# Causal attention, a gated layer and routed experts on one core: half of the attention pairs copy P by DMA into a float32r tile and transpose it from there, two banks in one run

## The chip, the cores and the metric

One core of a Trainium2 chip runs the whole kernel. The metric is the device time of one execution in microseconds (us), as a median of several runs. TensorE (PE) does the matmuls, VectorE (DVE), ScalarE (ACT) and GpSimd (POOL) work on their results, SyncE (SP) issues the DMAs.

## What is computed

Three layers in a row, here with b = 0..3, 12 heads of 64, 448 positions and a width of 768:

```python
scores = where(causal, q @ k.T / 8, -1e9)            # layer 1: plain causal attention
x = softmax(scores) @ v                              # heads side by side: (4, 448, 768)

theta = x @ w_theta                                  # layer 2
y = w_tok_r @ (x * cos(theta)) + w_tok_i @ (x * sin(theta))
u = x + y;  x = u + relu(u @ w_ch)

w = softmax of the two largest of x @ w_gate         # layer 3: 4 experts, each one head of 64
for e in range(4):
    out += (w[e] where e was chosen) * (softmax(causal(x @ wq[e] @ (x @ wk[e]).T / 8)) @ (x @ wv[e]) @ wo[e])
```

## The kernel before

Everything is held transposed (features on partitions, the 448 positions along the row), and heads come in pairs: two heads of 64 fill 128 partitions. Layer 1 has six pairs for each b (`attn1`), layer 3 two pairs of experts for each b (`attn2`): 32 pairs in all. Between them `dense1` does layer 2 and the projections of layer 3.

The dense matmuls take float32r operands, each number split into a high and a low part of which three products are summed (`mm3`). Their weights are converted once for b = 0, written to a scratch in HBM, and read back from there for every b as tiles `unit`, six buffers of them, by DMAs in SP's queue. SP's queue also brings q and k of a pair (`raw`) and v (`vt`), and stores the result.

One call of `pair` does attention for two heads:

- `scores([2])`: the scores of the third block of 128 positions of both heads, float32 matmuls on one half of the array's rows for each head, side by side, into two banks `sc`. Then the scores of the last 64 positions of both heads together, then `scores([1, 0])`.
- `softmax`: VectorE adds the mask and finds the row's extreme, ScalarE takes the exponential and the sum, into P (`pa`, one tile for each head, and `pc` for the last positions). `norm` scales P by the reciprocal sums, on GpSimd or ScalarE.
- P is transposed in blocks of 128 by 128, four to a PSUM bank `tp`, four banks a pair (`banks`), 16 transposes: P's block is the stationary operand, the identity the moving one, both float32. Each bank is copied to a tile `ph` by ScalarE or VectorE as soon as its four are there.
- `av`: 16 float32 matmuls, each head on one half of the array's columns, and the result is split into high and low (`hl`).

The order of instructions on each engine is not that of the program. `Plan` collects steps with a due time and costs of its own (`cost`, `LATENCY`, `DMA_RATE`), and `issue` writes each engine's queue in the order of a list schedule: at each point an engine takes the ready step of the earliest due time whose buffers are free. The table `K` sets the due times. On the chip each queue then runs strictly in the order written. Attention for the next b is meant to stand between the matmuls of the dense layers of this b. Since all instructions are written by one helper, all have line 478 in the profile, and tiles tell them apart.

Of the kernel before, what the change touches and what calls it, by code (L numbers as in the profile page):

```python
# [23 lines left out]
P = 128  # L24
# [94 lines left out]
ANY = {"cmb", "cv"}  # L119
# [6 lines left out]
class Plan:  # L126
# [16 lines left out]
    def cost(self, engine, name, out, ins, kw):  # L143
        n = out.width if isinstance(out, View) else 0
        psum = any(v.root.psum for v in ins)
        if engine == "tensor":
            n = ins[1].width
            if name != "matmul":
                return 109.0
            if ins[1].dtype != F32:  # L150
                return max(52.0, 8.0 + 0.43 * n)
            if self.mode(ins, name):
                return 8.0 + 0.86 * n
            return 16.0 + 1.72 * n
# [36 lines left out]
    def add(self, engine, name, *args, **kw):  # L191
# [8 lines left out]
        if isinstance(self.block, Step) and self.block.engine == engine:  # L200
            step = self.block
            step.cost += cost
        else:
            step = Step()
            step.calls, step.engine, step.cost, step.options, step.done = [], engine, cost, [], []
            step.deps, step.users, step.tiles, step.fresh = {}, [], [], []
            step.soft, step.heirs = {}, []
            step.order = len(self.steps)
            step.due = self.due
            step.lag = 0.0  # L210
            step.mode = self.mode(ins, name) if engine == "tensor" else 0
# [100 lines left out]
    def issue(self):  # L312
# [62 lines left out]
        while count < len(self.steps):  # L375
# [13 lines left out]
            for e in order:  # L389
# [4 lines left out]
                for x in avail[e]:  # L394
# [86 lines left out]
class Engine:  # L481
# [3 lines left out]
    def __getattr__(self, method):  # L485
# [3 lines left out]
K = {"path": 1.62, "hop": -40.0, "slack": 10.0, "war": 300.0, "ahold": 41360.0, "f1": 0.03, "f2": 0.91, "f3": 1.13,  # L489
# [7 lines left out]
def dense_sparse_attention_kernel(ctx: ExitStack, tc: tile.TileContext, qk, v, w64, w32, wo, wvg, wtok, out):  # L497
# [10 lines left out]
            "qp": 3, "v2": 4, "pa": 3, "pc": 2, "ph": 3, "cmb": 2, "st": 9, "gt": 2, "sm": 2}  # L508
# [13 lines left out]
    pool.identity(ident)  # L522
    mask = const([512], F32, "mask")
# [82 lines left out]
    def pair(raw, vts, gate, dest, due, gap, tag=lambda name: name):  # L606
# [21 lines left out]
        def scores(chunks):  # L628
            banks = [pst("sc") for _ in range(2)]
            plan.group()  # L630
            at = 0
            for c in chunks:
                n = 128 * (c + 1)
                for j in range(2):
                    pe.matmul(banks[j][:, at:at + n], qs[j][:, 128 * c:128 * c + 128], ks[j][:, :n], start=True, stop=True)
                at += n
            plan.end_group()
            at = 0
            for c in chunks:
                n = 128 * (c + 1)  # L640
                for j in range(2):
                    softmax(banks[j][:, at:at + n], part(j, c), n, mask[:, 512 - n:512], 2 * (2 - c) + j)
                at += n
# [9 lines left out]
        scores([2])  # L653
# [5 lines left out]
        scores([1, 0])  # L659
# [3 lines left out]
        def blk(who, c, kc):  # L663
            if who == 2:
                return pc[:, kc * 128:kc * 128 + 128]
            return ps[who][:, SECS[c] + kc * 128:SECS[c] + kc * 128 + 128]
# [3 lines left out]
        parts = [sbt([1024], F32, tag("ph")) for _ in range(2)]  # L670
        for t, i, blocks in banks:
            tp = pst("tp")
            at = 0
            for who, c, kc in blocks:
                if who == 2:
                    pe.transpose(tp[:, at:at + 128], blk(who, c, kc), ident)
                    at += 128
                else:
                    place = tp[:, at:at + 256].rearrange("p (h j d) -> p h j d", h=2, j=2)
                    pe.transpose(place[:, :, who], blk(who, c, kc), ident)  # L680
                    at += 256 * who
            plan.copy(parts[t][:, 512 * i:512 * i + 512], tp)
# [11 lines left out]
        plan.completes(o_[:, :S])  # L694
        if dest is not None:
            plan.copy(dest, o_[:, :S])
        h_ = sbt([S], F32R, "hl")
        l_ = sbt([S], F32R, "hl")
# [7 lines left out]
    def attn1(b, due0, gap):  # L706
        for pr in range(H // 2):
# [22 lines left out]
            xhl[b, pr] = pair(fetch, [vt[:, j] for j in range(2)], None, xp, due, gap, tag)  # L730
# [162 lines left out]
    def attn2(b, due0, gap):  # L893
        qps, v2, g7 = st2[b]
        hl = []
        for r in range(2):
            due = due0 + r * gap
            hl.append(pair(lambda: qps[r], [v2[r][:, :, j] for j in range(2)], g7[:, r, :], None, due, gap))
        banks = K["wom"] if b == B - 1 else K["wo2"] if b == B - 2 else "a"
        names = {"a": "av", "m": "mm", "s": "sc", "t": "tp", "v": "av"}  # L900
        for m in range(NK):
# [6 lines left out]
            o = pst(names[banks[m % len(banks)]])  # L908
            i = 0
# [4 lines left out]
            ob = sbt([S], F32, "xt" if b == B - 1 else "cmb")  # L914
# [70 lines left out]
```

## Time and profile before

| | |
|---|---|
| Time, median of 3 runs | 675.54 us (674.79 to 676.07) |
| The profiled execution's own time | 675.52 us |
| Its span from the first to the last instruction | 673.7 us |
| Instructions | 11076, of them 3752 matmuls |
| TensorE busy | 645.6 us of the span |
| Granted clock of TensorE, mean | 0.991 |

The profiled execution stands at the median of the runs, so its parts can be added up to a time without any scaling. A busy TensorE in the profile means that some matmul is between its start and its modelled end; neighbours overlap, so what one costs in a row of them is read from the distance between starts, or from the chain of waits, where each piece holds the time that it alone took.

### The profile page before, as it was taken

The page shows a single profiled execution, that of the slowest core. Times are in us where ns is not written, and L with a number is a line of the kernel's source. Part 1 is how long each engine was busy: PE and PEld are TensorE (multiplying, and loading weights), DVE is VectorE, ACT ScalarE, POOL GpSimd, SP SyncE. Part 2 cuts the span into 40 slices and gives each one's busy share as a digit, 9 for nine tenths or more (in the row PEclk, how much of TensorE's full clock was granted, in tenths as well). Part 3 has the DMA queues.
Part 4 walks back from the last instruction along what each step waited for, and adds up shares of the span by engine and source line. Part 5 has one row for each costly group of instructions (what it writes and reads, how often), then busy time and mean ns, then how long its engine had stood idle before and what let it go on. Part 6 is the DMA issues. An engine that isn't in the chain of part 4 may idle for free.

```text
span 673.7 us, 11076 instructions
## 1 busy us (share of the span) xinstructions
PE 645.6 (96%) x3752; PEld 522.7 (78%) x3752; DVE 418.3 (62%) x1301; ACT 391.0 (58%) x977; POOL 111.3 (17%) x215
## 2 busy tenths in 40 slices
PE   7997679999999999999999999999999999999997
PEld 5664468778797879877887778788788888997875
DVE  4999999998955586543435677354633457434251
ACT  5999788768724482344557677543555364105374
POOL 3542212222200211000102134100100012001010
PEclk8999979999999999999999999999999999999999
DMA  8845630345788624245536442415541750063243
GB/s 332 282 140 193 241 125 29 110 150 176 273 257 277 220 100 149 88 139 162 166 93 236 154 141 67 139 46 173 148 132 48 229 172 23 24 220 116 64 156 134
DMA packets 46184, 103.13 MB, mean 153 GB/s; under 512 B 4784, under 2 KB 16560, under 8 KB 46128
## 3 DMA queue, kind: packets, MB, share of 16 engines
q1 hardware_dynamic: 46128, 102.43, 46.8%
q8 instruction: 29, 0.48, 0.3%
q14 instruction: 27, 0.22, 0.1%
HBM read 81.15 MB, written 21.26 MB: 152 GB/s over the span
## 4 chain that ended last, share of the span: by engine, by line
PE 83%; DVE 8%; ACT 6%; issue 1%; DMA 1%; POOL 0%; ACTq 0%; POOLq 0%; DVEq 0%
PE mm L478 54%; PE av L478 10%; PE sc L478 9%; PE tp L478 7%; PE cv L478 3%; ACT pa L478 2%; DVE cmb L478 2%; DVE zt L478 1%; ACT zn L478 1%; DVE pa L478 1%; DVE c L478 1%; DVE zn L478 1%; DMA unit<-scr 1%; ACT ph L478 1%; ACT pc L478 1%
## 5 line engine op out<-in xcount | busy, mean ns | idle before, releaser
L478 PE MATMUL mm<-zt,unit 128*128 128x448 f32 x720 | 161.1, 374 | 0.0
L478 ACT ACTIVATE pa<-pa,st 128x384 f32<-128x384 f32 (+2 forms) x262 | 125.3, 492 | 43.1 <-DVE st L478 37.6
L478 PEld LDWEIGHTS mm<-zt,unit 128*128 128x128 f32 x720 | 132.5, 188 | 17.3 <-issue 5.7
L478 PE MATMUL mm<-wt,zn 128*128 128x448 f32 x504 | 124.2, 380 | 0.5 <-ACT zn L478 0.5
L478 PE MATMUL mm<-hl,unit 128*128 128x448 f32 x432 | 103.5, 385 | 6.1 <-DVE zt L478 4.3
L478 PEld LDWEIGHTS mm<-wt,zn 128*128 128x128 f32 x504 | 90.4, 188 | 11.5 <-issue 2.0
L478 PEld LDWEIGHTS mm<-hl,unit 128*128 128x128 f32 x432 | 81.0, 193 | 20.2 <-DVE zt L478 5.5
L478 DVE CUSTOM_DVE_ANT_0 pa<-sc,mask 128x384 f32<-128x384 f32 (+1 forms) x174 | 67.0, 419 | 44.3 <-PE sc L478 37.6
L478 POOL TENSOR_SCALAR pa<-pa,st 128x256 f32<-128x256 f32 (+2 forms) x86 | 46.5, 550 | 256.9 <-DVE st L478 176.8
L478 ACT ACTIVATE ph<-tp 128x512 f32<-128x512 f32 x103 | 56.8, 593 | 44.4 <-PE tp L478 44.1
L478 PE MATMUL sc<-raw 64*128 64x384 f32 (+3 forms) x336 | 69.5, 437 | 2.0 <-DVE st L478 1.7
L478 PE MATMUL tp<-ident,pa 128*128 128x128 f32 x348 | 58.6, 275 | 5.0 <-POOL pa L478 4.1
L478 PEld LDWEIGHTS tp<-ident,pa 128*128 128x128 f32 x348 | 42.9, 141 | 13.0 <-POOL pa L478 5.3
L478 ACT ACTIVATE pc<-pc,st 128x448 f32<-128x448 f32 x56 | 37.4, 667 | 20.0 <-DVE st L478 19.5
L478 PE MATMUL av<-ph,vt 128*64 128x448 f32 (+3 forms) x384 | 46.8, 386 | 2.1 <-ACT xt L478 2.1
L478 PEld LDWEIGHTS av<-ph,vt 128*64 128x64 f32 x384 | 25.4, 136 | 27.4 <-issue 11.2
L478 PEld LDWEIGHTS sc<-raw 64*128 64x128 f32 (+1 forms) x336 | 33.8, 189 | 14.3 <-issue 5.9
L478 DVE TENSOR_TENSOR zn<-cv,zn 128x512 fp32r<-128x512 f32 (+1 forms) x48 | 29.8, 620 | 23.5 <-ACT zn L478 23.4
L478 PE MATMUL mm<-unit,zt 128*128 128x260 f32 (+1 forms) x288 | 40.7, 289 | 0.9 <-DMA unit<-scr 0.9
L478 ACT ACTIVATE zn<-cv 128x512 fp32r<-128x512 f32 (+1 forms) x36 | 19.5, 541 | 34.8 <-PE cv L478 34.7
L478 PEld LDWEIGHTS mm<-unit,zt 128*128 128x128 f32 (+1 forms) x288 | 36.1, 175 | 4.0 <-issue 1.8
L478 POOL MEMSET pc<- 128x64 f32 x32 | 5.0, 161 | 169.5 <-PE tp L478 169.4
(115 smaller groups left out, 893.9 us busy)
## 6 DMA issues: line engine op xcount, KB each, us to landing
unit<-scr SPq DMA_DIRECT2D x96, 384.0 KB, 3.5
scr<-unit SPq DMA_DIRECT2D x32, 384.0 KB, 3.2
raw<-qk SPq DMA_DIRECT2D x24, 480.0 KB, 4.3
c<-w SPq DMA_DIRECT2D x24, 384.0 KB, 3.3
vt<-v SPq DMA_DIRECT2D x24, 256.0 KB, 3.3
unit<-scr SPq DMA_DIRECT2D x18, 260.0 KB, 3.2
c<-scr SPq DMA_DIRECT2D x18, 256.0 KB, 2.8
out<-cmb SPq DMA_DIRECT2D x18, 224.0 KB, 2.7
```

Of the source, the lines that this page charges most:

```text
L478: getattr(getattr(self.nc, engine), name)(*args, **kw)
```

## The change

For 16 of the 32 pairs (layer 1 of b = 2 and 3, layer 3 of b = 1 and 2; `moved` is true), the blocks of P are copied by DMA from `pa` and `pc` into a new tile `bits` of type float32r, eight blocks to a tile and five DMAs to a tile, on SP's queue. The transposes read `bits` with a float32r identity, and write two banks `tp` in one run of eight; a pair has two such runs. The bits copied are those of the float32 numbers. `bits` takes its buffers from the tag `ph`, which has four of them now, before three. The other 16 pairs transpose as they did.

The rest concerns the order: the planner's price of a transpose, of a run on the new tile and of a change between parts of the array; a rule `stay`, by which TensorE, once it has done a step that uses a part of the array, prefers another such step that is ready and due within 4510 ns; `tp` banks taken in any order; some tiles claimed at an earlier step, and the six matmuls of the last projection kept together; and the table `K`, whose due times are all different. `joined` is false at both calls, so `scores` makes the same matmuls as before.

```diff
-ANY = {"cmb", "cv"}
+ANY = {"cmb", "cv", "tp"}
...
             if name != "matmul":
-                return 109.0
+                return 62.0 if ins[0].dtype != F32 else 109.0
...
+            if engine == "tensor" and name != "matmul" and ins[0].dtype != F32:
+                step.cost += 100.0
...
+                    if e == "tensor" and mode:
+                        if not s.mode:
+                            if pick is None:
+                                pick = x
+                            if due <= pick[0] + K["stay"]:
+                                continue
+                            break
+                        if pick is None or due <= pick[0] + K["stay"]:
+                            pick = x
+                        break
...
-                        end += 150.0
+                        end += 180.0
...
-K = {"path": 1.62, "hop": -40.0, "slack": 10.0, "war": 300.0, "ahold": 41360.0, "f1": 0.03, "f2": 0.91, "f3": 1.13,
-     "a0": 6370.0, "start": 56960.0, "d1": 25850.0, "g1": 13100.0, "gap": 15170.0, "gap1": 0.04, "gap2": -0.75, "len0":
...
+K = {"stay": 4510.0, "path": 1.7, "hop": -660.0, "slack": 10.0, "war": 300.0, "ahold": 36380.0, "f1": -0.01, "f2": 0.72,
+     "f3": 1.65, "a0": 4960.0, "start": 56770.0, "d1": 26990.0, "g1": 13110.0, "gap": 17410.0, "gap1": 0.36, "gap2":
...
-            "qp": 3, "v2": 4, "pa": 3, "pc": 2, "ph": 3, "cmb": 2, "st": 9, "gt": 2, "sm": 2}
+            "qp": 3, "v2": 4, "pa": 3, "pc": 2, "ph": 4, "cmb": 2, "st": 9, "gt": 2, "sm": 2}
...
+    identr = const([P], F32R, "identr")
+    dve.tensor_copy(identr, ident)
...
+            for p in ps:
+                plan.claim(p)
...
+        srcs = [x.rearrange("p (n j) -> p n j", j=128) for x in (ps[0], ps[1], pc)]
...
+        def move(t):
+
+            bits = sbt([8, 128], F32R, tag("ph"))
+            at = {}
+            x = 0
+            for i in (1, 0):
+                for who in range(3):
+                    todo = [(SECS[c] // 128 + kc if who < 2 else kc, (who, c, kc)) for w, c, kc in sets[t, i] if w == who]
+                    todo.sort()
+                    while todo:
+                        n = len(todo)
+                        step = todo[1][0] - todo[0][0] if n > 1 else 1
+                        while any(todo[k][0] != todo[0][0] + k * step for k in range(n)):
+                            n -= 1
+                        first = todo[0][0]
+                        sp.dma_start(bits[:, x:x + n].f32(), srcs[who][:, first:first + (n - 1) * step + 1:step])
+                        for k in range(n):
+                            at[todo[k][1]] = bits[:, x + k]
+                        x += n
+                        todo = todo[n:]
+            return lambda *key: at[key]
+
+        sets = {(t, i): blocks for t, i, blocks in banks}
+        groups = [((0, 1), (0, 0)), ((1, 1), (1, 0))] if moved else [((t, i),) for t, i, _ in banks]
+        for group in groups:
+            where = move(group[0][0]) if moved else block
+            tps = [pst("tp") for _ in group]
+            plan.group()
+            for tp, key in zip(tps, group):
+                at = 0
+                for who, c, kc in sets[key]:
+                    place = tp[:, at:at + 128]
+                    if who < 2:
+                        place = tp[:, at:at + 256].rearrange("p (h j d) -> p h j d", h=2, j=2)[:, :, who]
+                    pe.transpose(place.bitcast(F32R) if moved else place, where(who, c, kc), identr if moved else ident)
+                    at += 128 if who == 2 else 256 * who
+            plan.end_group()
...
+            plan.claim(parts[t])
+            for tp, (t, i) in zip(tps, group):
+                plan.copy(parts[t][:, 512 * i:512 * i + 512], tp)
...
-            xhl[b, pr] = pair(fetch, [vt[:, j] for j in range(2)], None, xp, due, gap, tag)
+            xhl[b, pr] = pair(fetch, [vt[:, j] for j in range(2)], None, xp, due, gap, False, b > 1, tag)
...
-            hl.append(pair(lambda: qps[r], [v2[r][:, :, j] for j in range(2)], g7[:, r, :], None, due, gap))
+            hl.append(pair(lambda: qps[r], [v2[r][:, :, j] for j in range(2)], g7[:, r, :], None, due, gap, False, 0 < b < B - 1))
```

## Rows read from the trace of the kernel before

**Rows 1.** The page, busy time of each engine: us, share of the span, instructions.

```profile
PE 645.6 (96%) x3752; PEld 522.7 (78%) x3752; DVE 418.3 (62%) x1301; ACT 391.0 (58%) x977; POOL 111.3 (17%) x215
```

**Rows 2.** Busy time by stretch; then granted clock, DMA share, GB/s.

```profile
60.00:112.00 52.00, 38.90 (x200) 29.12 (x198) 51.19 (x140) 40.61 (x92) 7.83 (x12) 0.93 0.41 139
...
215.00:340.00 125.00, 125.00 (x706) 104.16 (x704) 70.51 (x200) 63.44 (x155) 16.21 (x33) 1.00 0.48 156
...
380.00:480.00 100.00, 100.00 (x581) 81.56 (x578) 55.31 (x157) 56.92 (x135) 19.25 (x33) 1.00 0.38 119
```

**Rows 3.** TensorE's waits from 215 to 630 us: total, times, longest.

```profile
PE cv L478 <- DVE zn L478: 1.2, 1, 1.2
PE mm L478 <- DMA unit<-scr: 0.9, 1, 0.9
```

**Rows 4.** The page, the chain that ended last: shares by engine.

```profile
PE 83%; DVE 8%; ACT 6%; issue 1%; DMA 1%; POOL 0%; ACTq 0%; POOLq 0%; DVEq 0%
```

**Rows 5.** That chain in order of time, 290 to 375: start, us, what.

```profile
296.99 10.80 PE mm L478 x52
...
309.28 0.87 PE tp L478 x8
...
313.99 1.88 PE av L478 x16
315.87 0.85 PE sc L478 x8
...
340.58 4.93 DMA unit<-scr
345.52 0.04 issue
...
347.43 1.44 PE mm L478 x12
```

**Rows 6.** Timeline of TensorE around those two blocks: start, us, shape, count.

```profile
296.92 10.87 PE L478 MATMUL mm<-zt,unit 128*128 128x448 f32 x52
...
346.92 1.95 PE L478 MATMUL mm<-unit,zt 128*128 128x260 f32 x12
```

**Rows 7.** Groups by shape, matmuls (PE) and weight loads (PEld): busy us, mean ns.

```profile
L478 PE MATMUL tp<-ident,pa 128*128 128x128 f32 x348 | 58.6, 275 | 5.0 <-POOL pa L478 4.1 <-ACT ph L478 0.9
...
L478 PE MATMUL sc<-raw 64*128 64x128 f32 x96 | 9.6, 271 | 0.0
...
L478 PEld LDWEIGHTS mm<-zt,unit 128*128 128x128 f32 x720 | 132.5, 188 | 17.3 <-issue 5.7
...
L478 PEld LDWEIGHTS tp<-ident,pa 128*128 128x128 f32 x348 | 42.9, 141 | 13.0 <-POOL pa L478 5.3 <-ACT ph L478 2.0 <-issue 1.4
...
L478 PEld LDWEIGHTS sc<-raw 64*128 64x128 f32 x288 | 25.5, 189 | 13.3 <-issue 5.9 <-DVE st L478 4.1 <-DVE cmb L478 0.5
L478 PEld LDWEIGHTS av<-ph,vt 128*64 128x64 f32 x384 | 25.4, 136 | 27.4 <-issue 11.2 <-ACT pa L478 2.3 <-ACT xt L478 2.3
```

**Rows 8.** The tile vt, SP's issues: ns min/median/max, first and last start.

```profile
L478 SPq DMA_DIRECT2D vt<-v x24: 327/333/861, 1.7 to 498.0; - x24
```

**Rows 9.** What SP's queue waited for, 260 to 630 us: total, times, longest.

```profile
SPq L478 <- PE mm L478: 214.3, 86, 30.7
SPq L478 <- PE av L478: 47.1, 16, 8.0
```

**Rows 10.** DMA issues: count, KB each, median us from issue to landing.

```profile
raw<-qk SPq DMA_DIRECT2D x24, 480.0 KB, 4.3
...
out<-xt SPq DMA_DIRECT2D x6, 224.0 KB, 2.4
```

**Rows 11.** Timeline: the last scaling of a P and the transposes after it.

```profile
348.16 0.67 ACT L478 ACTIVATE pc<-pc,st 128x448 f32<-128x448 f32 x1
...
350.18 1.03 PE L478 MATMUL tp<-ident,pa 128*128 128x128 f32 x8
...
621.93 0.68 ACT L478 ACTIVATE pa<-pa,st 128x128 f32<-128x128 f32 x2
...
623.40 0.82 PE L478 MATMUL tp<-ident,pa 128*128 128x128 f32 x6
```

More of the change, by code (lines that the diff above doesn't have):

```diff
@@ L604, in dense_sparse_attention_kernel, with pair @@
     SECS = [0, 128, 384]
-    def pair(raw, vts, gate, dest, due, gap, tag=lambda name: name):
+    def pair(raw, vts, gate, dest, due, gap, joined, moved, tag=lambda name: name):
         plan.due = due
@@ L628, in scores @@
         def scores(chunks):
-            banks = [pst("sc") for _ in range(2)]
+            own = [pst("sc") for _ in range(2)]
+            more = [pst("tp") for _ in range(2)] if len(chunks) == 3 else own
+            where = {}
+            for j in range(2):
+                for c in chunks:
+                    at = 384 if (c == 0 and len(chunks) == 3) else 256 if c == 0 else 0
+                    where[j, c] = (more if c == 1 else own)[j][:, at:at + 128 * (c + 1)]
             plan.group()
-            at = 0
             for c in chunks:
-                n = 128 * (c + 1)
                 for j in range(2):
-                    pe.matmul(banks[j][:, at:at + n], qs[j][:, 128 * c:128 * c + 128], ks[j][:, :n], start=True, stop=True)
-                at += n
+                    pe.matmul(where[j, c], qs[j][:, 128 * c:128 * c + 128], ks[j][:, :128 * (c + 1)], start=True, stop=True)
             plan.end_group()
-            at = 0
+            for p in ps:
+                plan.claim(p)
             for c in chunks:
-                n = 128 * (c + 1)
                 for j in range(2):
-                    softmax(banks[j][:, at:at + n], part(j, c), n, mask[:, 512 - n:512], 2 * (2 - c) + j)
-                at += n
+                    n = 128 * (c + 1)
+                    softmax(where[j, c], part(j, c), n, mask[:, 512 - n:512], 2 * (2 - c) + j)
         def norm(a, b_, items):
@@ L651, in norm @@
                 plan.scale(p, p, rec[:, col:col + 1])
-        scores([2])
+        scores([2, 1, 0] if joined else [2])
         norm(0, 2, [(part(j, 2), j) for j in range(2)])
@@ L658, in pair @@
         softmax(sc_[:, :S], pc[:, :S], S, mask3, 6)
-        scores([1, 0])
+        if not joined:
+            scores([1, 0])
         norm(2, 7, [(pc[:, :S], 6)] + [(part(j, c), 2 * (2 - c) + j) for c in (1, 0) for j in range(2)])
         plan.due = due + K["f2"] * gap
[L663 to L666, printed above, removed]
         banks = [(0, 1, [(0, 2, 0), (1, 2, 0), (2, 3, 0), (2, 3, 3)]), (1, 1, [(2, 3, 1), (0, 2, 2), (1, 2, 2), (2, 3, 2)]),
@@ L669, in pair @@
                  (0, 0, [(0, 0, 0), (1, 0, 0), (0, 1, 0), (1, 1, 0)]), (1, 0, [(0, 1, 1), (1, 1, 1), (0, 2, 1), (1, 2, 1)])]
[L670 to L682, printed above, removed]
+        srcs = [x.rearrange("p (n j) -> p n j", j=128) for x in (ps[0], ps[1], pc)]
@@ new lines, in pair, with block @@
+        parts = [None, None]
+        def block(who, c, kc):
+            return srcs[who][:, kc] if who == 2 else srcs[who][:, SECS[c] // 128 + kc]
+        def move(t):
[18 more added lines that the diff above has]
+            return lambda *key: at[key]
@@ new lines, in pair @@
+        sets = {(t, i): blocks for t, i, blocks in banks}
[13 more added lines that the diff above has]
+            plan.end_group()
+            t = group[0][0]
+            if parts[t] is None:
+                parts[t] = sbt([1024], F32, tag("ph"))
+            plan.claim(parts[t])
+            for tp, (t, i) in zip(tps, group):
+                plan.copy(parts[t][:, 512 * i:512 * i + 512], tp)
@@ L694, in pair @@
         plan.completes(o_[:, :S])
+        h_ = sbt([S], F32R, "hl")
+        l_ = sbt([S], F32R, "hl")
+        for t in (h_, l_) + ((dest,) if dest is not None else ()):
+            plan.claim(t)
         if dest is not None:
             plan.copy(dest, o_[:, :S])
-        h_ = sbt([S], F32R, "hl")
-        l_ = sbt([S], F32R, "hl")
         plan.copy(h_, o_[:, :S])
@@ L908, in attn2 @@
             o = pst(names[banks[m % len(banks)]])
+            ob = sbt([S], F32, "xt" if b == B - 1 else "cmb")
+            plan.group()
             i = 0
@@ L913, in attn2 @@
                     i += 1
-            ob = sbt([S], F32, "xt" if b == B - 1 else "cmb")
+            plan.end_group()
+            plan.claim(ob)
             plan.copy(ob, o[:, :S])
```

6 rows, old and new, of the table K are left out of this document.

## The prediction

> **What bounds the kernel now.** I read the page's busy shares first, then the stretches, then what TensorE waits for, then the chain of waits. TensorE is busy 96% of the span [rows 1], but that share is a mean over two unlike parts. Until 112 us VectorE or ScalarE is full and TensorE is not (38.90 of 52 us in the second stretch, at a mean granted clock of 0.93). From 112 us on TensorE has no air: 125.00 of 125 us between 215 and 340, 100.00 of 100 between 380 and 480, at a granted clock of 1.00, while VectorE and ScalarE are little over half busy [rows 2]. In all the time from 215 to 630 us it has two waits worth the name, 2.1 us in sum [rows 3], and 83% of the chain that ended last is TensorE [rows 4]. So in this part a microsecond of TensorE's own work is a microsecond of the span, and a chain of the other engines costs nothing until TensorE has run out of other work.
>
> The pairs that the change moves are those of attn1 for b = 2 and 3 (12) and of attn2 for b = 1 and 2 (4). Their transposes lie between about 276 and 624 us, all in the full part. That is why I cost the change on TensorE first.
>
> **1. Cheaper transposes.** 16 pairs with 16 transposes each are 256. The chain shows eight in a row as 0.87 us, 0.109 each, and the next matmuls follow without a step between [rows 5]. The trace has no float32r transpose. Bounds: above, the same 0.109. Below, the spacing of float32r matmuls carried down to 128 columns: 52 of 448 columns take 10.80 us (0.208 each), 12 of 260 columns take 1.44 us (0.120 each); the timeline gives their widths [rows 5, 6]. The slope is 0.088 / 188 = 0.00047 us a column, and 132 columns less than 260 make 0.120 - 0.062 = 0.058 us. What decides between the bounds is whether the moving side or the weight load spaces transposes out. A transpose's matmul lasts 275 ns, the same as a float32 pass of 128 columns (271 ns): the moving identity is a float32 stream, and that halves. Its weight load lasts 141 ns, where 128 columns of a float32r matmul last 188 ns and 64 columns 136 ns [rows 7]: it is already as short as one of half the columns, so it is not what holds a transpose at 0.109. I take 0.060, near the lower bound: 256 x 0.049 = **12.5 us less** (bounds 0 and 13.1).
>
> The Trainium skill (TensorE: Matmul & The Clock Gate, LDWEIGHTS (loading the stationary operand)) has a rule that speaks against this: a load takes its columns divided by 1.2, in ns, so an estimate of 107 ns for 128 columns whatever the type, and no transpose could follow another in less. The rows agree for the matmuls' loads against those of 64 columns (52 ns more for 64 columns more) and differ for the transposes' own; by the rule this step would give nothing, and it is a rival below.
>
> **2. Two banks in one run.** There are now 32 runs of 8 transposes, each waiting for both "tp" banks and for five landings. Price for entering a run: nothing by the float32 runs above; the planner in the diff charges itself 0.1 us, 3.2 us over 32 runs. The chain has steps of 0.04 us named issue right after a landing released TensorE [rows 5]. One such step a run, 0.05 us, is my value: **1.6 us more** (bounds 0 and 3.2). The evictions, of 512 columns each, stay the same in number and engine; they are covered because VectorE and ScalarE have free time here [rows 2].
>
> **3. The copies.** Each moved pair issues 10 DMAs, five a run, 160 in all, which carry 1 MB a pair and 16.8 MB over the kernel. All go through SP's queue, between the weight loads, raw and vt. An issue takes SP 0.33 us (vt), so 53 us in sum, of a queue that waits far longer than that for TensorE to free buffers (214.3 us from 260 to 630 us) [rows 8, 9]: the issues themselves are free. Not free is the landing: 2.4 us for 224 KB, 4.3 for 480 KB [rows 10]. A run's five copies carry 512 KB, so 4.3 us is my value, 2.4 the lower bound and 4.3 + 5 x 0.33 = 6.0 the upper one, if all five go out after the last block is scaled. In this time the transposes stand in TensorE's queue, and what is behind them (matmuls of the dense layers) stands still too, if they come up early. Are they early now? At 350.18 the second eight transposes start 1.35 us after the last scaling of that P ended (348.16 + 0.67), at 623.40 it is 0.8 us (621.93 + 0.68) [rows 11]. Of the 16 pairs five have less than 1.4 us (350, 359, 371, 523 and 623 us, of which the first and the last stand in the rows), two have 4.1, the other nine more than 4.3. If the new order kept these distances, and with both runs only after the whole P, TensorE would stand 2.9 + 3.7 + 3.2 + 3.5 + 3.5 + 0.4 = 17.2 us. But the order is written anew, by a planner that counts a landing of 2.2 us plus the bytes for each copy, and the full part has matmuls to put before a run: ahead of 307 us a block of 52 stands there, 10.80 us long [rows 5]. The tight places are near the ends of the batches, where the next dense layer waits for the last pair. I let a fifth be paid: **3.4 us more** (bounds 0 and 17.2).
>
> Buffers: a pair now holds four of four "ph" tiles in place of two of three, two of them only from the copies to the transposes. P itself ("pa", "pc") comes free when the copy has landed rather than when the transposes are done, which with the distances above is about the same moment. I give neither a price.
>
> **4. The rest of the diff.** "stay" lets TensorE, once it works on a part of the array, take another such step that is ready. From 294 to 526 us each av run has a scores run at its side already (one of them in the rows, av x16 with sc x8 after it) [rows 5], so there is nothing to join: zero, and at most the few av runs that stand alone outside. The claims, groups and the due times (K) change the order everywhere, the first 112 us too. There TensorE stands 13 us in the second stretch [rows 2], and a new order may lose or win some of it: zero, with 4 us either way in the range. "identr" is one small copy, before VectorE has work.
>
> **Sum.** The profiled execution took 675.52 us (span 673.7, the rest around it), as good as the median of the runs, 675.54. 675.5 - 12.5 + 1.6 + 3.4 = **668.0 us**, 1.1% less. With the bounds of the entering price, the late runs between 0 and 7 and the early part, this case alone reaches from 661 to 674.
>
> **Rivals.**
> *The weight load spaces the transposes (0.10).* If a float32r transpose's load is one of 188 ns like those of the float32r matmuls, and not one of 141 [rows 7], the load can't hide behind a shorter moving side, spacing stays at 0.109, and the change does not do what it says: 675.5 + 1.6 + 3.4 = 680.5, slower. For it: the operand's type is that of the matmuls with the long load. Against: the float32 scores' loads of 128 columns last 189 ns as well, so type is not what makes the transposes' load short. The rule of the Trainium skill named above is this case.
> *Copies land late (0.12).* Place: SP's queue, which runs strictly in the order written. Weight loads in it wait for a buffer that TensorE frees, up to 30.7 us long [rows 9]; a copy behind one goes out only then, and a load behind a copy that waits for its P goes out late: at 340.58 one such load already held TensorE [rows 3, 5]. With the 17.2 us of step 3 paid in full: 675.5 - 12.5 + 1.6 + 17.2 = 681.8, slower. It decides from 10.9 us on, 0.34 us for each of the 32 runs. Against: five of 16 pairs are tight, the others have 4 us and more, and DMA engines are busy under half of the time in most stretches [rows 2].
> *The early part is ordered worse, by more than the gain (0.04).* It would take 9 us more idle time before 112 us, where 13 us are idle now: about 677. Nothing in the profile points to it.
>
> The Trainium skill (DMA: Bandwidth & Descriptors, Anatomy of one DMA — SWDGE (gpsimd) path) gives 2.0 us plus the bytes at 436 GB/s for a DMA of another issuing path, an estimate of 3.2 us for 512 KB. The row of 480 KB at 4.3 us is longer [rows 10]; by the page's figure the late time of step 3 would shrink by about 1 us for each tight run.
>
> **How the numbers follow.** The likeliest case has 0.74, the three rivals 0.10, 0.12 and 0.04. A measurement of this kernel can tell about 0.2% (1.4 us) from no change, so faster means under 674.2 and slower over 676.9. The likeliest case lies under 674.2 but for a few in a hundred; a half-paid rival (part of the spacing, half of the late time) comes out near no change or below. That makes faster 0.77, within 0.2% 0.06, slower 0.17. The range is from 660 to 677: below it lies only a gain with no late run and a better early part, above it the two rivals that are paid in full.
>
> **What the profile after would show.** Step 1: 256 transposes on the new tile, a run of eight in 0.5 us in place of 0.87, weight loads near 140 ns; at 0.87 and 188 ns the first rival holds. Step 2: the distance from the last transposes' start to the next matmul as in the float32 runs, or 0.1 us more. Step 3: waits of TensorE for DMA on the copied tile, few and short in sum; over 11 us of them, or more waits for unit loads, and the second rival holds. Step 4: the same number of av and scores runs side by side, and about 13 us idle from 60 to 112 us. The forecast is wrong if TensorE's busy time from 215 us on does not fall by 10 us, or if its idle time there rises by as much.

## The result, and the profile after

The changed kernel takes 683.58 us (681.81 to 684.78, four runs), the kernel before 675.16 us beside it (674.56 to 676.07): a ratio of 1.0122, interval 1.0100 to 1.0144. It is 8.4 us slower; 668.0 us were forecast, faster, in a range of 660 to 677. Its profiled execution took 683.88 us, span 682.1, mean granted clock 0.986.

Busy time of each engine on the page after, as [rows 1]:

```profile
PE 646.9 (95%) x3752; PEld 520.8 (76%) x3752; DVE 441.4 (65%) x1327; ACT 377.2 (55%) x954; POOL 115.0 (17%) x211
```

TensorE is not less busy than before (645.6 us), although 256 of its matmuls became cheaper, and the time in which it is not busy grew from 28.1 us (673.7 - 645.6) to 35.2 (682.1 - 646.9).

The three stretches of [rows 2], after:

```profile
60.00:112.00 52.00, 40.62 (x194) 31.03 (x192) 47.96 (x127) 39.41 (x92) 12.64 (x14) 0.84 0.43 141
215.00:340.00 125.00, 123.47 (x710) 99.31 (x709) 80.62 (x240) 69.22 (x178) 20.61 (x41) 1.00 0.56 179
380.00:480.00 100.00, 98.76 (x579) 78.95 (x578) 64.44 (x178) 56.45 (x141) 16.41 (x31) 1.00 0.55 173
```

Where TensorE had no air, it now stands 1.2 to 1.5 us in a stretch, and in the early one, which holds no moved pair, the granted clock fell from 0.93 to 0.84.

What TensorE waits for from 215 to 630 us, as [rows 3]:

```profile
PE mm L490 <- DVE zt L490: 1.6, 2, 1.0
PE sc L490 <- DVE st L490: 1.4, 2, 1.0
PE cv L490 <- DVE zn L490: 1.4, 1, 1.4
PE tp L490 <- DMA ph<-pa: 0.8, 2, 0.5
PE mm L490 <- DVE v L490: 0.5, 1, 0.5
```

The copies hold a transpose up twice, 0.8 us in all. Most of the new waits are for VectorE, for tiles that the change does not touch: a sign that another order, not the copies, is being waited in.

The planner chooses the engine of some steps, too, and VectorE is 23.1 us busier than before (441.4, 418.3). The copies of the banks `tp` to `ph` account for it; first before, then after:

```profile
L478 ACT ACTIVATE ph<-tp x103: 569/596/609, 16.3 to 660.2; 128x512 f32<-128x512 f32 x103
L478 DVE COPY ph<-tp x25: 675/685/692, 16.0 to 648.8; 128x512 f32<-128x512 f32 x25
```

```profile
L490 ACT ACTIVATE ph<-tp x66: 570/597/621, 18.3 to 667.1; 128x512 f32<-128x512 f32 x66
L490 DVE COPY ph<-tp x62: 672/684/693, 15.1 to 634.5; 128x512 f32<-128x512 f32 x62
```

Of 128 such copies 37 went from ScalarE to VectorE, at 0.685 us each. Step 2 of the prediction took them to "stay the same in number and engine". Over the whole span TensorE waits some 22 us for VectorE in place of 10. No run moves these copies alone, so how much of that is theirs stays open.

The transposes on the new tile by shape, beside [rows 7], and one run of eight in the timeline with its weight loads, beside [rows 5, 11]:

```profile
L490 PE MATMUL tp<-identr,ph 128*128 128x128 f32 x256 | 27.6, 248 | 0.9 <-DMA ph<-pa 0.8
L490 PEld LDWEIGHTS tp<-identr,ph 128*128 128x128 f32 x256 | 24.8, 140 | 9.8 <-issue 5.4 <-DMA ph<-pa 1.3 <-ACT zn L490 0.5
```

```profile
309.36 0.74 PEld L490 LDWEIGHTS tp<-identr,ph 128*128 128x128 f32 x8 [0.55 <-issue]
309.37 0.88 PE L490 MATMUL tp<-identr,ph 128*128 128x128 f32 x8
```

The load is 140 ns, as forecast, but the matmul lasts 248 ns where float32 lasts 275, and eight of them take 0.88 us from the first start to the last end: (0.88 - 0.248) / 7 = 0.090 us from one to the next, where [rows 11] give (1.03 - 0.275) / 7 = 0.108. The median distance over the 224 neighbours is 85 ns, before 109. The forecast had 60. From the start of a run's last transpose to the start of the next matmul it is 85 ns as well (median of the 32 runs), after the float32 runs of the kernel before 28.

The copies: SP's issues (ns min/median/max), their landing, and what SP's queue waited for from 260 to 630 us, beside [rows 8, 10, 9]:

```profile
L490 SPq DMA_DIRECT2D ph<-pa x128: 465/562/1578, 258.3 to 631.1; - x128
L490 SPq DMA_DIRECT2D ph<-pc x32: 586/624/2181, 262.1 to 629.1; - x32
```

```profile
ph<-pa SPq DMA_DIRECT2D x64, 128.0 KB, 2.3
...
ph<-pa SPq DMA_DIRECT2D x64, 64.0 KB, 2.0
ph<-pc SPq DMA_DIRECT2D x32, 128.0 KB, 2.6
```

```profile
SPq L490 <- PE mm L490: 114.6, 56, 30.9
SPq L490 <- ACT pa L490: 43.2, 18, 7.8
SPq L490 <- POOL pa L490: 18.6, 9, 7.9
```

An issue takes 0.56 us, not the 0.33 of vt, so five are 2.8 us of SP's queue before the last can begin its 2.0 to 2.6 us. SP now waits 61.8 us (43.2 and 18.6) for P to be scaled, with everything behind the copy waiting too.

### The profile page after: what moved, and what is told of

Read it like the earlier page. It is cut to its first block, busy times and chain, and to the rows that moved or that the text cites. A ratio compares the mean times of both kernels' runs of the same rounds, so it can differ in the third digit from the quotient of the medians.

```text
span 682.1 us, 11518 instructions
## 1 busy us (share of the span) xinstructions
PE 646.9 (95%) x3752; PEld 520.8 (76%) x3752; DVE 441.4 (65%) x1327; ACT 377.2 (55%) x954; POOL 115.0 (17%) x211
## 5 line engine op out<-in xcount | busy, mean ns | idle before, releaser
L490 ACT ACTIVATE pa<-pa,st 128x128 f32<-128x128 f32 (+2 forms) x271 | 128.0, 489 | 74.1 <-DVE st L490 60.4
L490 PE MATMUL mm<-wt,zn 128*128 128x448 f32 x504 | 119.6, 380 | 0.0
L490 PEld LDWEIGHTS mm<-hl,unit 128*128 128x128 f32 x432 | 83.1, 197 | 25.3 <-DVE zt L490 8.6
L490 DVE CUSTOM_DVE_ANT_0 pa<-sc,mask 128x384 f32<-128x384 f32 (+1 forms) x174 | 65.5, 418 | 43.7 <-PE sc L490 28.7
L490 PE MATMUL sc<-raw 64*128 64x384 f32 (+3 forms) x336 | 71.5, 443 | 6.4 <-DVE st L490 6.4
L490 ACT ACTIVATE ph<-tp 128x512 f32<-128x512 f32 x66 | 37.4, 594 | 34.8 <-PE tp L490 29.5
L490 PEld LDWEIGHTS sc<-raw 64*128 64x128 f32 (+1 forms) x336 | 34.6, 190 | 24.1 <-DVE st L490 14.1
L490 DVE COPY ph<-tp 128x512 f32<-128x512 f32 x62 | 41.0, 685 | 17.7 <-PE tp L490 17.5
L490 PE MATMUL mm<-unit,zt 128*128 128x260 f32 (+1 forms) x288 | 38.2, 287 | 0.6 <-DVE v L490 0.5
L490 ACT ACTIVATION_READ_ACCUMULATOR pa<-pa,st 128x1 f32 x174 | 32.6, 187 | 0.0
L490 PEld LDWEIGHTS tp<-identr,ph 128*128 128x128 f32 x256 | 24.8, 140 | 9.8 <-issue 5.4
L490 ACT ACTIVATE zn<-cv 128x512 fp32r<-128x512 f32 (+1 forms) x30 | 16.4, 546 | 27.9 <-PE cv L490 27.8
```

Source lines behind the costliest of these rows:

```text
L490: getattr(getattr(self.nc, engine), name)(*args, **kw)
```

## The experiments

Times are medians of four to twelve runs, each beside runs of the kernel before on the same chip (674.7 to 675.7 us); "not busy" is the span minus TensorE's busy time on the page.

| kernel | us | ratio to before (interval) | not busy |
|---|---|---|---|
| before | 675.16 | 1 | 28.1 |
| the changed kernel | 683.58 | 1.0122 (1.0100 to 1.0144) | 35.2 |
| due_times_alone | 684.93 | 1.0152 (1.0137 to 1.0167) | 30.9 |
| claim_alone | 694.65 | 1.0291 (1.0276 to 1.0307) | 39.2 |
| old_due_times | 730.46 | 1.0813 (1.0795 to 1.0831) | 61.0 |
| same_order_f32 | 688.35 | 1.0204 (1.0188 to 1.0219) | 33.4 |
| direct_rounded | 671.42 | 0.9948 (0.9934 to 0.9961) | 27.3 |
| direct_all | 669.19 | 0.9919 (0.9904 to 0.9934) | 27.8 |
| order_without_copies | 680.68 | 1.0077 (1.0061 to 1.0094) | 32.4 |
| before_order_copies | 711.00 | 1.0537 (1.0519 to 1.0554) | 49.5 |
| copies_where_room | 676.64 | 1.0023 (1.0013 to 1.0032) | 31.3 |
| copies_in_halves | 749.75 | 1.1088 (1.1054 to 1.1122) | 79.3 |
| order_kept | 679.97 | 1.0077 (1.0055 to 1.0099) | 30.8 |
| last_pair_not_moved | 683.79 | 1.0132 (1.0115 to 1.0148) | 33.1 |

**due_times_alone.** The kernel before with the new table K and nothing else: no copy, no float32r transpose.

```diff
-K = {"path": 1.62, "hop": -40.0, "slack": 10.0, "war": 300.0, "ahold": 41360.0, "f1": 0.03, "f2": 0.91, "f3": 1.13,
...
+K = {'stay': 4510.0, 'path': 1.7, 'hop': -660.0, 'slack': 10.0, 'war': 300.0, 'ahold': 36380.0, 'f1': -0.01, 'f2': 0.72,
...
```

> The kernel before with the table K of the change and nothing else: no copies, all transposes in float32. Theory A (the loss is the order that the changed inputs of the planner write: more idle time, more changes between parts of the array): slower than before by 6 to 9 us, 681 to 685 us, with more than 24 us of idle TensorE. Theory B (the copies make the loss: their landing and their place in SP's queue push transposes, av and the last projections late): no copies, so as before, 675 us within 2.

It lost 10.2 us, more than the whole change. Its early stretch (the columns of [rows 2]):

```profile
60.00:112.00 52.00, 37.48 (x173) 28.20 (x170) 50.09 (x136) 36.29 (x80) 8.17 (x12) 0.84 0.43 138
```

In this stretch TensorE did 173 matmuls in place of 200 and had the clock of 0.84 that the changed kernel has. An order alone, for the same operations, moves the time by as much as is in question (some of them also change their engine: VectorE has 1307 instructions in place of 1301, GpSimd 209 in place of 215). That it is the order of the changed kernel, this run does not show.

**same_order_f32.** The changed kernel, its order and copies untouched, with the 256 transposes as float32 again.

```diff
+            if name == "transpose" and args[1].root.dtype == F32R:
+                args = [args[0].f32(), args[1].f32(), args[2].f32()]
```

> The changed kernel with the same order on every engine and the same copies; only the 256 transposes of the copied tile are done as float32. The trace of the changed kernel shows a run of eight at about 0.70 us where eight in float32 take 0.87. Theory A, which takes 0.17 us a run on a TensorE that is full there: slower than the changed kernel by 32 x 0.17 = 5.4 us, about 689 us. Step 1 as I priced it (0.049 us for each of 256) would make it 12.5 us, 696 us. If copies or other engines set the time (theory B in its strong form), the price of a transpose is hidden: under 2 us.

4.8 us more than the changed kernel, 5.2 when each is set against the kernel before beside it: that is what the cheaper transposes give, not 12.5.

**direct_rounded.** The order of before, no copies: in the same 16 pairs the masked scores, the exponentials and P are written as float32r, so P is rounded, and the transposes read it where it lies.

```diff
+            r = p.bitcast(F32R) if moved else p
...
-            act.activation(p, p, AF.Exp, bias=bias[:, col:col + 1], scale=-1.0, accum_out=sums[:, col:col + 1])
+            act.activation(r, p, AF.Exp, bias=bias[:, col:col + 1], scale=-1.0, accum_out=sums[:, col:col + 1])
...
-                plan.scale(p, p, rec[:, col:col + 1])
+                plan.scale(p.bitcast(F32R) if moved else p, p, rec[:, col:col + 1])
```

> The kernel before in its own order, no copies: in the same 16 pairs masked scores, exponentials and P are written as float32r (rounded, which changes the numbers a little) and transposed from there in float32r, one bank at a time. It isolates the cheap transpose, without copies and without a new order. Theory A, with 0.086 us a transpose and 0.02 to enter a run as the changed kernel's trace shows: 256 x 0.023 less 64 x 0.02 at most, 4.6 to 5.9 us less, 669 to 670 us. By step 1's price of 0.060: 12.5 us less, 662 us. If a float32r transpose were no cheaper in place: 675.

3.5 us less than before, faster than both kernels. Two runs now agree on the size of the first term, 3.5 and some 5 us.

**direct_all.** The same in all 32 pairs.

> The float32r transposes without copies, as in direct_rounded (scores, exponentials and P written as float32r, the order of before), now in all 32 pairs in place of 16. Theory A (a float32r transpose saves some 0.02 us where TensorE is full, and nothing where it is not): direct_rounded saved 3.5 us over 16 pairs, 0.22 a pair. The six pairs of layer 1 for b = 0 lie where TensorE has idle time, so they give little; 26 x 0.22 = 5.7 us, 669 to 670 us. Rival (step 1's price, 0.049 us a transpose): 675 - 25 = 650 us. Rival (the limit is elsewhere, and the 16 other pairs give nothing): 671.5, as with 16 pairs.

5.9 us less than before, the fastest version of this study. Its price: P is rounded in every pair.

**order_without_copies.** The changed kernel's order on every engine, its runs of two banks, its float32r transposes; only the 160 copies are left out, and the transposes read P directly, written as in direct_rounded.

```diff
+            if name == "transpose" and getattr(args[1], "src", None) is not None:
+                args = [args[0], args[1].src, args[2]]
+            if name == "dma_start" and isinstance(args[0], View) and args[0].root.tag == "ph":
+                continue
```

> The changed kernel with its exact order on every engine, its two banks in one run and its float32r transposes, but the 160 copies are left out: in the 16 pairs scores, exponentials and P are written as float32r and the transposes read them there. Theory A (what costs is the order that the edited planner writes, and the copies cost next to nothing once the order has made room for them): 681 to 684 us, as the changed kernel. Theory B (the copies cost although TensorE shows only 0.8 us of waits for them, through SP's queue, their landing and the buffers that they hold): 672 to 677 us.

680.68, just under the span of theory A and well above that of B. Against direct_rounded, which has the same transposes and no copies either, only the order differs (with it the engines that the planner chose and the runs of two banks): 1.0077 against 0.9948, 8.7 us. Against the changed kernel only the copies differ: 1.0077 against 1.0122, 3.0 us, which by the two intervals can be 1 to 5. The page of direct_rounded, then of order_without_copies:

```profile
PE 642.3 (96%) x3752; PEld 519.1 (78%) x3752; DVE 417.8 (62%) x1302; ACT 390.6 (58%) x977; POOL 111.8 (17%) x215
```

```profile
PE 645.0 (95%) x3752; PEld 520.4 (77%) x3752; DVE 440.4 (65%) x1327; ACT 378.4 (56%) x954; POOL 114.7 (17%) x211
```

The spans, 669.6 and 677.4 us, differ by 7.8; 5.1 of it is time in which TensorE is not busy (27.3 and 32.4), 2.7 is busy time. Where the first part lies, two stretches of direct_rounded and then of order_without_copies show:

```profile
215.00:630.00 415.00, 413.14 (x2424) 343.12 (x2425) 217.48 (x657) 212.16 (x521) 55.39 (x110) 1.00 0.44 136
630.00:690.00 60.00, 33.13 (x202) 25.72 (x201) 13.32 (x68) 22.73 (x61) 2.94 (x6) 0.96 0.26 82
```

```profile
215.00:630.00 415.00, 411.11 (x2405) 341.96 (x2404) 238.96 (x697) 200.70 (x499) 50.17 (x102) 1.00 0.45 136
630.00:690.00 60.00, 38.48 (x236) 28.72 (x235) 15.22 (x71) 23.68 (x62) 3.11 (x6) 0.96 0.25 82
```

From 215 to 630 us TensorE is not busy for 3.9 us in place of 1.9, from 630 us to the end of the span for 8.9 in place of 6.5; the rest is 1.1 more from 112 to 215 us and 0.4 less ahead of that. For the busy time the clock is enough: it stands at half for 23.3 us of the span in place of 16.5, which at 0.44 us lost for each (last section) is up to 3.0. Counted over the trace, TensorE has neither a matmul nor a weight load under way for 25.8 us in place of 19.8, and changes 172 times in place of 163 between steps on the whole array, on one half of its rows and on one half of its columns; av and scores runs stand side by side 18 times in place of 27. The start after such a change comes some 0.09 us later than without one (after a 448-column matmul 0.297 in place of 0.204, after a float32 transpose 0.203 in place of 0.109), so nine more cost 0.8 us.

**before_order_copies.** The opposite: the order of before, each engine's queue unchanged but for the copies in SP's, and in the 16 pairs the blocks of P copied right behind their scaling with seven DMAs a pair (one of the 16 blocks is transposed from P). All pairs share one set of copied tiles.

```diff
+                if moved:
+                    plan.steps[-1].copies = pc[:, :384] if col == 6 else p
...
+            self.nc.sync.dma_start(self._twin(v).bitcast(F32), v.ap())
```

> The kernel before in its own order, with 15 of the 16 blocks of P of the same 16 pairs copied by DMA right behind their scaling (seven DMAs a pair, one set of copied tiles) and transposed in float32r at the place where they stood. So the new chain meets the old distances between scaling and transposes. With landings of 2.0 to 2.6 us, as in the changed kernel's trace, and about 1 us of issue, some 3.5 us, the first runs of nine pairs are late by 0.8 to 3.5 us each, 26 us in sum: theory A and step 3 as written both expect 690 to 698 us, most of it as waits of TensorE for the copies. If queues matter more (theory B), over 700. If copies are hidden even here, about 670.

711.0, 36 us more than before: over the 690 to 698 of theory A and step 3, where the expectation put theory B. TensorE's waits:

```profile
PE tp L483 <- DMA bits<-pc: 11.6, 6, 5.3
PE tp L483 <- DMA bits<-pa: 8.9, 12, 1.8
```

They are 20.5 us, about the 17.2 of step 3. Not all of it is the distance between scaling and transposes: with the one set of tiles SP waits five times, 18.1 us in all, for transposes before it can copy, and no run has this test with more tiles. The rest of the loss is largely the clock, which stands at half for 54.6 us of the span, in the kernel before for 11.7 (worked out in the last section).

**copies_in_halves.** The changed kernel, each copy issued as two of 64 partitions: the same bytes, twice the issues.

```diff
+                for h in (0, 64):
+                    self.nc.sync.dma_start(args[0][h:h + 64], args[1][h:h + 64])
```

> The changed kernel with its exact order, but each of the 160 copies is issued as two of 64 partitions each: the same bytes, twice the issues, so a run's copies occupy SP's queue for some 2.5 us more. Theory A (in this order the copies are not on the path): 682.5 to 685.5 us, as the changed kernel. Theory B (the copies' issues in SP's queue are on the path, for the transposes or for the weight loads behind them): 2.5 us for each of the runs that have no room, 5 to 20 us in sum, 689 to 704 us, with waits of TensorE for DMA on the copied tiles.

66 us more than the changed kernel. Waits of TensorE, and three of them in the timeline:

```profile
PE tp L494 <- DMA ph<-pa: 42.7, 31, 3.2
```

```profile
410.83 0.43 PE L494 MATMUL tp<-identr,ph 128*128 128x128 f32 x3 [0.47 <-DMA ph<-pa]
...
416.66 0.38 PE L494 MATMUL tp<-identr,ph 128*128 128x128 f32 x2 [0.83 <-DMA ph<-pc]
418.96 0.69 PE L494 MATMUL tp<-identr,ph 128*128 128x128 f32 x6 [1.93 <-DMA ph<-pa]
```

TensorE now waits 32 times for a copy (31 of `pa`, one of `pc`, 43.5 us in all), and runs of eight transposes stand in pieces between landings. So the copies of the changed kernel are hidden with hardly any room to spare. Theory A of this run (the copies are off the path) falls, and the 5 to 20 us of theory B are far too few. What it shows of the changed kernel is that its order has room for 2.8 us of issues and 2 us of landing, and not for another five issues.

**old_due_times.** The changed kernel with the old table K.

> The changed kernel with everything in it but the table K, which is that of before (stay kept at 4510). Due_times_alone showed the new table to cost 10 us in the old planner; this puts the old table into the new one. Theory A (the new due times by themselves carry the cost of the order): 672 to 677 us. Theory B (no single edit carries it: table, claims and rules belong together, and a table that does not fit the planner's bookkeeping costs 10 to 20 us on top, as the claims did in claim_alone): 690 us and more. In between, 677 to 690, neither holds.

730 us, as theory B had it: in the new planner the new table is worth 47 us, in the old one it costs 10. So the table is not dear by itself; it belongs to the planner that it is used in. That it makes room for copies, which need some 5 us between the last scaling and the transposes, is likely but not shown.

**claim_alone.** The kernel before, with one line of the planner's bookkeeping.

```diff
+            for p in ps:
+                plan.claim(p)
```

> The kernel before with one line of the change and nothing else: both tiles of P are claimed when the scores are written instead of when the first softmax starts. No instruction is added, removed or changed, only the planner's bookkeeping and so the order. Theory A (orders written from other inputs than those that the table K fits are several us longer): slower by 5 us or more, 680 us or above. Theory B: 675 us, as before.

20 us more, with no operation added or removed; the planner writes another order and gives some steps to another engine (VectorE 1291 instructions in place of 1301, GpSimd 226 in place of 215). The order is that sensitive to what the planner believes.

**copies_where_room.** before_order_copies for six pairs alone, those whose transposes come over 4 us after the last scaling.

> before_order_copies (order of before unchanged, P copied by DMA right behind its scaling, float32r transposes in place) for six pairs alone, those with over 4 us from the last scaling to the first transposes: layer 1 b = 2 pair 1, b = 3 pairs 0, 2, 3, 4, layer 3 b = 2 pair 0. Theory A (the copies cost nothing where they have room, and all that was lost in before_order_copies was lost in the pairs without room): six pairs gain 0.22 to 0.34 us each, 672.7 to 673.7 us. Theory B (issue of 0.56 us for each copy in SP's queue and landing of 2 to 2.6 us make a chain of 5 us and more, which 4 us of room does not hide, or the copies hold up weight loads behind them): 675.5 to 682 us, with waits of TensorE for DMA on the copied tiles or on unit.

1.5 us slower than before; the six pairs should have saved 1.3. Theory B, at its lower end. In the trace one run of transposes waits 0.9 us for a copy, and TensorE's waits for the tiles `unit` went from 0.9 to 1.9 us.

**order_kept.** 18 pairs on copies, chosen by the planner's own estimate; the planner runs once without copies, and the times of that run become the due times of the second, so the order of before stays, except that the steps of a moved pair are due up to 12 us earlier to make room for its copies.

```diff
+        if self.times is not None:
+            for s in self.steps:
+                if s.key is not None:
+                    s.due, e = self.times[s.key]
+                    s.due -= s.pairof
```

> The kernel before with copies and float32r transposes, but the order of before kept: the planner runs twice, first as before, and then with the copies, taking each step's start in the first schedule as its due time and its engine from there, so that only what a copy delays moves. Pairs were put on copies one by one where the schedule did not get longer by it (18 pairs, among them 4 that the change does not move; 2 of layer 1 and 1 of layer 3 that it moves are left in float32). Transposes stay one bank at a time. Theory A: 18 x 16 x 0.023 us = 6.6 us less at most, less what the copies delay on the chip against the plan: 669 to 672 us, faster than both kernels. Theory B (the copies' landing and their place in SP's queue cost more than the transposes give): 676 us or more, with waits of TensorE for the copied tiles.

Theory A falls: 5 us slower than before, in the range of theory B. Even with an order made for few disturbances, the copies and what is moved for them eat the gain.

**last_pair_not_moved.** The end of the kernel, from the last dense layer on, is longer in the changed kernel; the last moved pair lies near it and is left unmoved here.

```diff
-            hl.append(pair(lambda: qps[r], [v2[r][:, :, j] for j in range(2)], g7[:, r, :], None, due, gap, False, 0 < b < B - 1))
+            hl.append(pair(lambda: qps[r], [v2[r][:, :, j] for j in range(2)], g7[:, r, :], None, due, gap, False, 0 < b < B - 1 and not (b == B - 2 and r == 1)))
```

> The changed kernel, with the last of its 16 moved pairs (the second of layer 3 for b = 2) left in float32 and not copied. The order of the first two thirds of the steps is the same. In the changed kernel this pair's second run of transposes starts at 633.6 us and its av ends at 637.9, after the dense matmuls, and the last 46 us hold 4.7 us of idle TensorE. If that pair's longer chain is what stretches the end: 3 to 5 us less than the changed kernel, 679 to 681 us. If the end is long because of the due times: within 1.5 us of 683.6.

No change (683.79): that pair is not what lengthens the end. From 630 us to the end of the span TensorE is not busy for 9.0 us in the changed kernel (52.1 - 43.10) where it was 5.3 (43.7 - 38.37); the rows stand in the next section.

## Why the prediction was wrong

The runs give a sum in place of the forecast's, each difference from two of them: 675.2, less 3.5 for float32r transposes (direct_rounded), plus 8.7 for the order with its runs of two banks (order_without_copies), plus 3.0 for the copies in this order (the changed kernel) is 683.4.

**Step 4, "The claims, groups and the due times (K) change the order everywhere ... zero, with 4 us either way", is the step that failed first.** The order costs 8.7 us, in which the engines that the planner chose and the runs of two banks are contained. The prediction looked for the order's price in the first 112 us alone, and there only for idle time. Part of it is there, but as clock: the granted clock of 60 to 112 us fell to 0.84, while TensorE is busy there for 40.62 us in place of 38.90. The idle time is in the full part, where each stretch shows a microsecond of new waits, for VectorE above all, and at the end. It was there to be asked: a list that keeps TensorE at 125.00 of 125 us [rows 2] has little to win from another one, and much to lose. Two things that the prediction counted on did not hold: the bank copies did not stay on their engines (37 of 128 moved to VectorE), and the av and scores runs side by side, to be the same in number, are 18 where they were 27. Why this order is the worse one is not shown. Likely it had to make room for a chain of about 5 us in each of 32 runs, and the room is paid elsewhere: without it the copies cost far more (before_order_copies, 36 us). But no run has an order that this planner writes with no copies to make room for. Which of the planner's edits costs how much stays open, too: due_times_alone, claim_alone and old_due_times show that they do not add up.

**Step 1, "I take 0.060 ... 12.5 us less", was mis-sized.** The direction is right, the transposes became cheaper, but by 3.5 to 5 us, as 0.109 became 0.085 and not 0.060. The weight load was rightly read as 140 ns; the error was to conclude from it that the moving side alone spaces the transposes, and to carry the slope from 448 and 260 columns down to 128. In the run of eight above the loads begin at the same 0.09 us distance as the matmuls, and neither the load's 140 ns nor the slope's 58 is that distance; what sets it, no run here separates. The Trainium skill (TensorE: Matmul & The Clock Gate, Back-to-back issue gap) says of a stream of load and matmul pairs that both operations set the spacing, some 81 ns for each matmul at 128 columns. The trace's 85 ns agrees. The first rival, in which a longer load keeps the spacing at 0.109 and the change gives nothing, falls with the 140 ns load, the 85 ns and same_order_f32. The rule that the prediction named beside it, from the Trainium skill (TensorE: Matmul & The Clock Gate, LDWEIGHTS (loading the stationary operand)), has 107 ns for such a load; these rows, 140 ns and a distance of 85, do not agree.

**Step 2, 1.6 us for entering a run, is about right, by luck: the price is at the other end.** A run of eight in float32r is left 0.057 us later than one in float32 (85 and 28 ns from the last transpose to the next matmul), 1.8 us for 32 runs. Seven distances shorter by 0.024 less this make 0.111 us a run and 3.6 us in all, where the two runs on the first term gave 3.5 and some 5.

**Step 3, "I let a fifth be paid: 3.4 us", came out at 3.0 (1 to 5), but not for its reason.** An issue costs 0.56 us, not 0.33; with the distances of before all is paid and more (36 us), and in the order that was written little, though not nothing. The second rival, copies landing late, needed 10.9 us or more of waits for DMA on the copied tile; there are 0.8. So it is not what happened, though copies_in_halves shows how near it is.

**The third rival, the early part ordered worse (0.04),** named the right kind of cause in one place only. In due_times_alone it is early; in the changed kernel the first matmul on `hl` of the next b starts at 215.2 us where it started at 211.9, 3.3 us, and the rest comes later, 3.7 us of new idle time after 630 us (9.0 and 5.3).

The test that the prediction set for itself gave the answer: TensorE's busy time from 215 us on was to fall by 10 us, and its idle time not to rise by as much. That stretch, in two pieces (the second runs past the end of the span), before, then after:

```profile
215.00:630.00 415.00, 412.58 (x2389) 343.37 (x2387) 217.92 (x656) 211.93 (x520) 55.39 (x110) 1.00 0.42 134
630.00:690.00 60.00, 38.37 (x240) 30.33 (x239) 13.42 (x68) 23.25 (x62) 2.91 (x6) 0.97 0.29 94
```

```profile
215.00:630.00 415.00, 409.95 (x2377) 339.04 (x2377) 240.43 (x704) 200.10 (x502) 50.23 (x101) 1.00 0.55 174
630.00:690.00 60.00, 43.10 (x269) 33.00 (x267) 15.69 (x72) 24.52 (x64) 3.26 (x7) 0.97 0.32 102
```

From 215 us to the end of the span TensorE's busy time rose by 2.1 us (450.95 to 453.05), and the time in which it is not busy from 7.8 to 14.1.

## What to carry to other kernels

Where an engine's queue is a fixed list that leaves it no idle time, price a change of the list first and the cheaper instruction second: run the new list with the old instructions, and the new instructions in the old list. A copy that stands between producer and consumer needs room in the list (here 5 x 0.56 us of issues and 2 us of landing), and it can cost more than the waits for it that the trace shows (3.0 us with 0.8 us of waits); if the producer can write the type that the consumer wants, and rounding there is allowed, the copy can go, which here is the only kind of version that won (direct_rounded and direct_all).

## What the runs showed of the hardware

A float32r transpose of 128 columns costs 85 ns in a run where a float32 one costs 109, with the same 140 ns load. Matmuls of 448 columns start 204 ns apart in float32r and 376 in float32, so what nearly halves there falls by a fifth here; and the next matmul after a run comes 85 ns after the last transpose's start in float32r, 28 in float32, so that short runs gain next to nothing (an estimate from these distances for a run of four: 340 ns in place of 355).

Splitting a copy by partitions gave nothing: the halves of the 128 KB copies landed in 2.1 us where the whole took 2.3, and each half's issue took SP as long as the whole's (medians 588 and 562 ns). The Trainium skill (DMA: Bandwidth & Descriptors, Rules for kernel authors) advises against two transfers to disjoint halves of the partitions, since they share the same engines; the 2.1 us against 2.3 agree with it.

An idle stretch costs twice. In the changed kernel, after 3.5 us in which TensorE waited, the next matmuls ran with the granted clock at half, that is 1.2 GHz, from 68.9 to 75.8 us:

```profile
70.02 6.54 PE L490 MATMUL mm<-hl,unit 128*128 128x448 f32 x18 [3.49 <-DVE zt L490]
```

Of these 18 matmuls of 448 columns, those at half clock start 0.373 us apart, where 52 at 2.4 GHz take 0.208 each [rows 5], so a microsecond at half clock loses 0.44 us. That explains the size of two losses. In before_order_copies TensorE has neither a matmul nor a load under way for 42.8 us in place of 21.7, and the clock is at half for 42.9 us more (54.6 and 11.7 of the span): 21.1 + 0.44 x 42.9 = 40.0, less the 3.5 of the transposes 36.5; measured, 36.3. In copies_in_halves, against the changed kernel, 71.9 in place of 28.5 and 62.9 in place of 19.2: 43.4 + 0.44 x 43.7 = 62.6 of the 66.2 measured.
